# Residual adds and moments re-divided over VectorE, ScalarE and GpSimd in the ends of two Fourier layers; a re-ordered cold stage

## The chip, the cores and the metric

The kernel runs on one core of one Trainium2 chip. The metric is device time in microseconds (us) of one execution; medians of several executions are given. Every execution of every kernel was fast (granted clock 0.997 to 0.999). Engines: PE is TensorE, PEld its weight loads, DVE is VectorE, ACT is ScalarE, POOL is GpSimd, SP is SyncE.

A ratio of two kernels is the mean time of one kernel's fast runs over the mean of the other's fast runs of the same rounds. It is therefore not quite the ratio of the medians that are quoted beside it.

## The reference, cut to what matters

Four layers act on x of 2048 tokens by 640 features, alternating A, B, A, B:

```python
x = x + A(layernorm(x), w_r, w_i)     # rfft2, times complex weights, irfft2
x = x + B(layernorm(x), mem0, Wq, Wk, Wv, Wo)   # 32 heads, 64 segments of 32 tokens with a carried memory
x = x + A(layernorm(x), w_r, w_i)
x = x + B(layernorm(x), mem0, Wq, Wk, Wv, Wo)
```

The Fourier transforms of A are matrix products with constant tables. The change touches two places: the **cold stage**, in which the first A layer reads x and folds its layer norm into scaled tables, and the **token stage**, the end of each A layer, which is run twice. There the inverse transform is done for 16 rows (groups of 128 tokens), each row gets its residual and its layer norm, and the normalized rows are handed to B.

## The kernel before

The token stage's work for one row. `psg` is the spectrum product, `psy` the inverse transform; the residual is added by two matmuls with the identity:

```python
def spectrum_d(s0):
    psg = pp.tile([128, 2, 512], FP32, name="psg", tag="pg", bufs=3)
    ...                                    # 6 matmuls
    nc.scalar.copy(out=Gs[s0 % 3], in_=psg[:, :, 0:NF])

def tokens(s0):
    ...
    psy = pp.tile([128, 2, 512], FP32, name="psy", tag="pg", bufs=3)
    for a in range(2):
        nc.tensor.matmul(psy[:, a, 0:320], lhsT=g["ident"][:], rhs=x[:, s0, a * 320:(a + 1) * 320], start=True, stop=False)
    ...                                    # 4 matmuls of the inverse transform
    if s0 < 15:
        nc.scalar.copy(out=halves(x[:, s0, :]), in_=psy[:, :, 0:320])
    ...

def stats(s0):                             # two bn_stats and a bn_aggr on VectorE
    _ln_stats(nc, st[s0 // 2], mv[s0 // 2], x[:, s0, :], s0 % 2)
```

Two rows share one inverse square root. ScalarE takes Ln and Exp of the variances, then GpSimd refines the result in four small operations after adding epsilon:

```python
nc.scalar.activation(out=r0, in_=mv[:, :nt, 1], func=ACTF.Ln, bias=eps_t[:, 0:1])
nc.scalar.activation(out=r0, in_=r0, func=ACTF.Exp, scale=-0.5)
small.tensor_scalar_add(out=t, in0=mv[:, :nt, 1], scalar1=LN_EPS)
small.tensor_tensor(out=t, in0=t, in1=r0, op=ALU.mult)
small.tensor_tensor(out=t, in0=t, in1=r0, op=ALU.mult)
small.tensor_scalar(out=t, in0=t, scalar1=-0.5, scalar2=1.5, op0=ALU.mult, op1=ALU.add)
small.tensor_tensor(out=t, in0=t, in1=r0, op=ALU.mult)
```

In this text the *statistics* of a row are the two `bn_stats`, one for each half of it; the *aggregate* (`bn_aggr`) joins them to the *moments*, which are the row's mean and variance; the *inverse* is the inverse square root of the variance, and the *norm* is the operation that subtracts the mean and multiplies by the inverse. PSUM is the memory into which TensorE writes its products.

In the main loop the program fixes the order of the instructions of TensorE, ScalarE and VectorE (`manual_schedule`), and in the timelines below each engine works its queue off in order, whatever else is ready.

Of the kernel before, what the change touches and what calls it, by code (L numbers as in the profile page):

```python
# [19 lines left out]
S, D = 2048, 640  # L20
NF = 321
# [86 lines left out]
def _ln_inverse(nc, pool, mv, nt, eps_t, small):  # L108
    rs = pool.tile([128, 4], FP32, name="lnrs", tag="lnrs", bufs=3)
    nb = pool.tile([128, 4], FP32, name="lnnb", tag="lnnb", bufs=3)  # L110
    t, r0 = rs[:, :nt], nb[:, :nt]
    nc.scalar.activation(out=r0, in_=mv[:, :nt, 1], func=ACTF.Ln, bias=eps_t[:, 0:1])
    nc.scalar.activation(out=r0, in_=r0, func=ACTF.Exp, scale=-0.5)
    if small is nc.vector:
        small.scalar_tensor_tensor(out=t, in0=mv[:, :nt, 1], scalar=LN_EPS, in1=r0, op0=ALU.add, op1=ALU.mult)
        small.scalar_tensor_tensor(out=t, in0=t, scalar=-0.5, in1=r0, op0=ALU.mult, op1=ALU.mult)
        small.scalar_tensor_tensor(out=t, in0=t, scalar=1.5, in1=r0, op0=ALU.add, op1=ALU.mult)
        return rs, nb
    else:
        small.tensor_scalar_add(out=t, in0=mv[:, :nt, 1], scalar1=LN_EPS)  # L120
        small.tensor_tensor(out=t, in0=t, in1=r0, op=ALU.mult)
    small.tensor_tensor(out=t, in0=t, in1=r0, op=ALU.mult)
    small.tensor_scalar(out=t, in0=t, scalar1=-0.5, scalar2=1.5, op0=ALU.mult, op1=ALU.add)
    small.tensor_tensor(out=t, in0=t, in1=r0, op=ALU.mult)
    return rs, nb
# [7 lines left out]
def _ln_apply(nc, pool, mv, xin, xout, nt, eps_t, on_dve=False):  # L133
    rs, nb = _ln_inverse(nc, pool, mv, nt, eps_t, nc.vector)
    if on_dve:
        _ln_scale(nc, mv, rs, xin, xout, nt)
        return
    nc.vector.scalar_tensor_tensor(out=nb[:, :nt], in0=mv[:, :nt, 0], scalar=-1.0, in1=rs[:, :nt], op0=ALU.mult, op1=ALU.mult)
    for t in range(nt):
        nc.scalar.activation(out=xout[:, t, :], in_=xin[:, t, :], func=ACTF.Identity, scale=rs[:, t:t + 1], bias=nb[:, t:t + 1])  # L140
# [54 lines left out]
class LayerA:  # L195
# [71 lines left out]
    def cold_raw(self, x_src, s3):  # L267
# [9 lines left out]
        for a, b in ((0, 2), (2, 4), (4, 8), (8, 12), (12, 16)):  # L277
            nc.sync.dma_start(out=x[:, a:b, :], in_=r16(x_src)[:, a:b, :])
            if a in (4, 8):
                nc.sync.dma_start(out=T[:, 2 * a - 8:2 * a, :], in_=g["cd"]["cT"][:, 2 * a - 8:2 * a, :])  # L280
        groups = [(0, 4), (4, 8), (8, 12), (12, 14), (14, 16)]
        by_act = (3, 7, 11)
        pp = tc.alloc_tile_pool(name=f"{self.lname}_ps1", bufs=8, space=PSUM)

# [3 lines left out]

        def scales(q):
            a, b = groups[q]  # L290
            sl, v = slice(a, b), mv[:, a:b, 1]
            small = nc.gpsimd if q < 4 else nc.vector
            nc.scalar.activation(out=r0[:, sl], in_=v, func=ACTF.Ln, bias=g["eps"][:, 0:1])
            nc.scalar.activation(out=r0[:, sl], in_=r0[:, sl], func=ACTF.Exp, scale=-0.5)
            n = b - 1 if b - 1 in by_act else b
            small.tensor_scalar_mul(out=mn[:, a:n], in0=mv[:, a:n, 0], scalar1=-1.0)
            if n < b:
                small.tensor_scalar_mul(out=mn[:, n:b], in0=nm[:, n:b], scalar1=D ** 0.5)
            t, r = rs[:, sl], r0[:, sl]
            if small is nc.gpsimd:  # L300
                small.tensor_scalar_add(out=t, in0=v, scalar1=LN_EPS)
                small.tensor_tensor(out=t, in0=t, in1=r, op=ALU.mult)
            else:
                small.scalar_tensor_tensor(out=t, in0=v, scalar=LN_EPS, in1=r, op0=ALU.add, op1=ALU.mult)
            small.tensor_tensor(out=t, in0=t, in1=r, op=ALU.mult)
            small.tensor_scalar(out=t, in0=t, scalar1=-0.5, scalar2=1.5, op0=ALU.mult, op1=ALU.add)
            small.tensor_tensor(out=t, in0=t, in1=r, op=ALU.mult)
            small.tensor_copy(out=mh[:, sl, 0], in_=mn[:, sl])
            small.tensor_tensor(out=mh[:, sl, 1], in0=mn[:, sl], in1=mh[:, sl, 0], op=ALU.subtract)

        def stats(t):
            for hlf in range(2):
                nc.vector.bn_stats(out=st[:, t % 2, hlf, :], in_=x[:, t, hlf * 320:(hlf + 1) * 320])
            nc.vector.bn_aggr(out=mv[:, t, :], in_=st[:, t % 2, :, :])

        def scale_tables(q):
            for t in range(*groups[q]):
                nc.vector.tensor_scalar_mul(out=Ts[:, t, :], in0=T[:, t, :], scalar1=rs[:, t:t + 1])
# [27 lines left out]
        with tc.manual_schedule(engines={nc.tensor.engine, nc.scalar.engine, nc.vector.engine, nc.gpsimd.engine}):  # L346
            act_stats(3)
            for t in (0, 1, 2):
                stats(t)
            scales(0)  # L350
            self.tables(mirror=False)
            self.load_mirror(0)
            act_stats(7)
            for t in (4, 5):
                stats(t)
            scale_tables(0)
            ps0 = matmuls(0)
            stats(6)
            scales(1)
            self.load_mirror(1)  # L360
            act_stats(11)
            for t in (8, 9):
                stats(t)
            scale_tables(1)
            empties(0, ps0, "AA")
            ps1 = matmuls(1)
            stats(10)
            scales(2)
            empties(0, ps0, "  AAA")
            for t in (12, 13):  # L370
                stats(t)
            scales(3)
            empties(1, ps1, "AA")
            scale_tables(2)
            ps2 = matmuls(2)
            stats(14)
            stats(15)
            scale_tables(3)
            scales(4)
            empties(1, ps1, "  AAA")  # L380
            ps3 = matmuls(3)
            scale_tables(4)
            empties(2, ps2, "AAADD")
            empties(3, ps3, "AADAD")
            ps4 = matmuls(4)
            empties(4, ps4, "DADAD")
# [183 lines left out]
    def tokens(self, x_dst, xn_dst, handoff=None):  # L570
# [17 lines left out]
        nm = wk.tile([128, 1], FP32, name="lnnm", tag="lnnm")  # L588

        def tokens(s0):  # L590
# [5 lines left out]
            for a in range(2):  # L596
                nc.tensor.matmul(psy[:, a, 0:320], lhsT=g["ident"][:], rhs=x[:, s0, a * 320:(a + 1) * 320], start=True, stop=False)
            nc.tensor.matmul(psy[:, 0, 0:320], lhsT=Ti[:, s0, 0, :], rhs=G[:, 0, 0:320], start=False, stop=False)
            nc.tensor.matmul(psy[:, 0, 0:320], lhsT=Ti[:, s0, 0, :], rhs=G[:, 1, 0:320], start=False, stop=True)
            nc.tensor.matmul(psy[:, 1, 0:320], lhsT=Ti[:, s0, 0, :], rhs=G[:, 0, 320:0:-1], start=False, stop=False)  # L600
            nc.tensor.matmul(psy[:, 1, 0:320], lhsT=Ti[:, s0, 1, :], rhs=G[:, 1, 320:0:-1], start=False, stop=True)
            if s0 < 15:
                nc.scalar.copy(out=halves(x[:, s0, :]), in_=psy[:, :, 0:320])
            else:
                nc.scalar.activation(out=halves(x[:, s0, :]), in_=psy[:, :, 0:320], func=ACTF.Identity, accum_out=nm[:])
# [5 lines left out]
        def stats(s0):  # L611
            _ln_stats(nc, st[s0 // 2], mv[s0 // 2], x[:, s0, :], s0 % 2)

        def act_stats(s0):
            m, scr = mv[s0 // 2][:, s0 % 2, :], Gs[1].rearrange("p a b -> p (a b)")[:, 0:D]
            nc.scalar.mul(out=nm[:], in_=nm[:], mul=-D ** -1.5)
            nc.scalar.activation(out=scr, in_=x[:, s0, :], func=ACTF.Square, scale=D ** -0.5, bias=nm[:, 0:1], accum_out=m[:, 1:2])
            nc.gpsimd.tensor_scalar_mul(out=m[:, 0:1], in0=nm[:], scalar1=-D ** 0.5)

        def inverse(q, small):  # L620
            rs[q], _ = _ln_inverse(nc, wk, mv[q], 2, g["eps"], small)

        def norm(q):
            xno = xna[:, 2 * q:2 * q + 2, :]
            _ln_scale(nc, mv[q], rs[q], x[:, 2 * q:2 * q + 2, :], xno, 2)
            nc.sync.dma_start(out=xnd[:, 2 * q:2 * q + 2, :], in_=xno)

        with tc.manual_schedule(engines={nc.tensor.engine, nc.scalar.engine, nc.vector.engine}):
            moved, late = [], []
            for i in range(16 + 1):  # L630
                for f in moved:
                    f()
                moved = []
                if late:
                    late.pop(0)()
                last = i >= 13
                if i >= 2 and last:
                    stats(i - 2)
                if i >= 5 and i % 2 == 1:
                    norm((i - 5) // 2)  # L640
                if i >= 2 and not last:
                    stats(i - 2)
                if i < 16:
                    spectrum_d(i)
                if 1 <= i <= 16:
                    tokens(i - 1)
# [14 lines left out]
                if i >= 8 and i % 4 < 3:  # L661
                    n = i % 4
                    jobs = handoff.rows_out(handoff.rows_in(pp, xna, i // 4 - 2, 2 * n), n != 1 and i < 16)
                    if n == 1:
                        late = jobs
                    else:
                        moved = jobs
            act_stats(15)
# [274 lines left out]
class _BOut:  # L943
# [13 lines left out]
    def run(self, wk, oT_of, psx, first=(), n_first=0):  # L957
        nc = self.tc.nc
        for t in range(S // 128):
# [11 lines left out]
            if self.xnd is not None:  # L971
# [3 lines left out]
                _ln_apply(nc, wk, mv, xo, xno, 1, self.g["eps"], on_dve=True)  # L975
# [496 lines left out]
class _FastOut:  # L1472
# [10 lines left out]
    def run(self, x, lhs_of, psx, first, n_first, pa, xns, check, acc, flag_col):  # L1483
        nc, nxt = self.tc.nc, self.nxt
        early = {t: c for c, t in enumerate((3, 5) if nxt is not None else (3, 5, 7, 9, 11))}
        for t in range(16):
# [10 lines left out]
            else:  # L1497
# [4 lines left out]
                _ln_apply(nc, self.g["ln"], mv, x[:, t:t + 1, :], xns[t % 3].unsqueeze(1), 1, self.g["eps"], on_dve=True)  # L1502
# [169 lines left out]
def make_globals(ctx, tc, Wq, Wk, Wv, Wo, mem0):  # L1672
# [8 lines left out]
    nc.vector.memset(g["eps"][:], LN_EPS)  # L1681
    g["floor"] = sp.tile([128, 1], FP32, name="floor")
# [127 lines left out]
```

## Time and profile before

The kernel before takes 1558.79 us (three runs, 1558.63 to 1559.9).

| stretch | us | what is in it |
|---|---|---|
| cold stage | 26.6 | VectorE without a gap until its last scaled table |
| spectrum, not changed | 47.5 | TensorE |
| token stage, first and second | 42.4 each | TensorE early, three engines near full later |
| attention, not changed | 674.0, first | TensorE 99.9% busy |

First the operations of one inverse in the token stage (line, engine, operation, names, shapes, count; busy us and mean ns of one; idle time before), then VectorE's wait for their result (us in total, number of waits, longest; up to 107.1, that is without the wait of 0.71 before the norm of rows 12 and 13).

```profile
L120 POOL TENSOR_SCALAR lnrs<-lnmv 128x2 f32<-128x2 f32 x7 | 1.7, 241 | 20.1 <-DVE lnmv L105 20.1
L121 POOL TENSOR_TENSOR lnrs<-lnrs,lnnb 128x2 f32<-128x2 f32 x7 | 1.4, 196 | 6.8 <-ACT lnnb L113 6.2 <-ACT lnnm L616 0.7
...
L123 POOL TENSOR_SCALAR lnrs<-lnrs 128x2 f32<-128x2 f32 x7 | 1.3, 191 | 0.6
```

```profile
DVE A1tok_S L130 <- POOL lnrs L124: 3.4, 3, 2.1
```

### The profile page before, as it was taken

The page shows a single profiled execution, that of the slowest core. Times are in us where ns is not written, and L with a number is a line of the kernel's source. Part 1 is how long each engine was busy: PE and PEld are TensorE (multiplying, and loading weights), DVE is VectorE, ACT ScalarE, POOL GpSimd, SP SyncE. Part 2 cuts the span into 40 slices and gives each one's busy share as a digit, 9 for nine tenths or more (in the row PEclk, how much of TensorE's full clock was granted, in tenths as well). Part 3 has the DMA queues.
Part 4 walks back from the last instruction along what each step waited for, and adds up shares of the span by engine and source line. Part 5 has one row for each costly group of instructions (what it writes and reads, how often), then busy time and mean ns, then how long its engine had stood idle before and what let it go on. Part 6 is the DMA issues. An engine that isn't in the chain of part 4 may idle for free.

```text
span 1557.3 us, 36583 instructions
## 1 busy us (share of the span) xinstructions
PE 1531.2 (98%) x14482; PEld 1077.5 (69%) x14483; DVE 815.5 (52%) x2414; ACT 771.7 (50%) x2251; POOL 234.4 (15%) x327
## 2 busy tenths in 40 slices
PE   7999999999999999999999999999999999999998
PEld 5776666666666666777777776666666666667775
DVE  7873545665556555633367545655556545553111
ACT  5584555556555565511127655556555565562000
POOL 3520111112111121100034101112111121110000
PEclk9999999999999999999999999999999999999999
DMA  4681344444433433645114523443533434327241
GB/s 171 222 304 30 111 151 140 137 140 134 160 131 137 148 125 145 203 116 169 51 50 165 174 69 125 137 150 124 179 123 137 146 125 171 124 101 233 75 132 51
DMA packets 168694, 214.88 MB, mean 138 GB/s; under 512 B 8128, under 2 KB 134088, under 8 KB 168512
## 3 DMA queue, kind: packets, MB, share of 16 engines
q1 hardware_dynamic: 167936, 210.15, 41.0%
q8 instruction: 115, 1.88, 0.5%
q0 software_dynamic: 576, 2.30, 0.4%
q14 instruction: 67, 0.55, 0.1%
HBM read 167.32 MB, written 45.10 MB: 136 GB/s over the span
## 4 chain that ended last, share of the span: by engine, by line
PE 94%; DVE 2%; ACT 1%; DMA 1%; issue 1%; POOL 1%; SPq 0%; DVEq 0%; POOLq 0%; ACTq 0%
PE psv L1201 19%; PE psk L1135 18%; PE psx L1481 18%; PE psq L1135 18%; PE pso L1285 4%; PE pss L1211 4%; PE ab L427 2%; PE psg L585 1%; PE psl L1238 1%; PE psq L1159 1%; PE X L458 1%; PE psu L519 1%; PE psm L911 1%; DMA bB_S<-in_B_Wk_dram 1%; PE psg L1642 1%
## 5 line engine op out<-in xcount | busy, mean ns | idle before, releaser
L1135 PEld LDWEIGHTS <-bB_S 128*128 128x128 bf16 x3180 | 261.7, 97 | 181.6 <-DMA bB_S<-in_B_Wk_dram 1.1
L1194 DVE CAST bB_S<-psk 128x495 bf16<-128x495 f32 (+3 forms) x320 | 191.8, 599 | 281.2 <-PE psk L1135 276.7
L1481 PE MATMUL psx<-Wo_sb,bB_S 128*128 128x320 bf16 x2048 | 288.7, 299 | 0.1
L1214 ACT ACTIVATE bB_S<-pss 128x269 bf16<-128x269 f32 (+5 forms) x576 | 208.4, 386 | 138.2 <-PE pss L1211 137.9
L1481 PEld LDWEIGHTS <-bB_S 128*128 128x128 bf16 x2048 | 196.8, 98 | 73.9 <-DVE bB_S L1299 0.7
L1179 ACT ACTIVATE bB_S<-psq 128x96 bf16<-128x96 f32 x300 | 152.4, 508 | 172.2 <-PE psq L1135 172.2
L1254 POOL TENSOR_TENSOR bB_S<-bB_S,bB_S 128x535 f32<-128x535 f32 x90 | 111.7, 1255 | 795.2 <-DVE bB_S L1246 762.2
L1299 DVE TENSOR_TENSOR bB_S<-pso,bB_S 128x480 bf16<-128x480 f32 (+1 forms) x320 | 193.1, 603 | 55.6 <-PE pso L1285 44.9
L1215 DVE TENSOR_TENSOR bB_S<-bB_S,maskf 128x269 bf16<-128x269 bf16 (+5 forms) x576 | 159.4, 290 | 114.4 <-ACT bB_S L1214 114.4
L1203 ACT CAST bB_S<-psv 128x512 bf16<-128x512 f32 (+1 forms) x288 | 162.6, 564 | 80.9 <-PE psv L1201 80.9
L1201 PE MATMUL psv<-bB_S,B1hT_S 128*128 128x256 bf16 x1360 | 168.8, 272 | 0.0
L1201 PE MATMUL psv<-bB_S,B2hT_S 128*128 128x256 bf16 x1360 | 168.8, 272 | 0.0
L1135 PE MATMUL psk<-B2hT_S,bB_S 128*128 128x495 bf16 (+3 forms) x800 | 164.2, 343 | 0.0
L1135 PE MATMUL psk<-B1hT_S,bB_S 128*128 128x495 bf16 (+3 forms) x800 | 164.2, 343 | 0.0
L1135 PE MATMUL psq<-B1hT_S,bB_S 128*128 128x495 bf16 (+5 forms) x780 | 156.1, 336 | 0.6 <-DMA bB_S<-in_B_Wk_dram 0.5
L1135 PE MATMUL psq<-B2hT_S,bB_S 128*128 128x495 bf16 (+5 forms) x780 | 156.1, 336 | 0.5 <-DMA bB_S<-in_B_Wk_dram 0.5
L1201 PEld LDWEIGHTS <-B2hT_S 128*128 128x128 bf16 x1360 | 129.8, 98 | 24.3
L1201 PEld LDWEIGHTS <-B1hT_S 128*128 128x128 bf16 x1360 | 129.8, 98 | 24.3
L1211 PE MATMUL pss<-bB_S 128*128 128x132 bf16 (+8 forms) x1152 | 137.5, 219 | 0.0
L1211 PEld LDWEIGHTS <-bB_S 128*128 128x128 bf16 x1152 | 95.4, 97 | 55.1
L1285 PE MATMUL pso<-bB_S,bB_S 128*128 128x132 bf16 (+8 forms) x1152 | 118.6, 219 | 0.2
L1285 PEld LDWEIGHTS <-bB_S 128*128 128x128 bf16 x1152 | 89.7, 98 | 32.2 <-DVE oTmf L1300 1.8
(293 smaller groups left out, 1422.0 us busy)
## 6 DMA issues: line engine op xcount, KB each, us to landing
bB_S<-Rd SPq DMA_DIRECT2D x124, 535.0 KB
oTx_d<-bB_S SPq DMA_DIRECT2D x60, 512.0 KB
bB_S<-oTx_d SPq DMA_DIRECT2D x46, 512.0 KB
bB_S<-in_B_Wq_dram SPq DMA_DIRECT2D x32, 320.0 KB
bB_S<-in_B_Wk_dram SPq DMA_DIRECT2D x32, 320.0 KB
bB_S<-in_B_Wv_dram SPq DMA_DIRECT2D x32, 320.0 KB
Wo_sb<-in_B_Wo_dram SPq DMA_DIRECT2D x4, 1280.0 KB
B1wv_S<-in_B_Wv_dram SPq DMA_DIRECT2D x10, 512.0 KB
```

The source lines that it names most:

```text
L1135: nc.tensor.matmul(ps, lhsT=w[:, ch, hh * 128:(hh + 1) * 128], rhs=src[:, ch, lo:hi], start=(ch == 0), stop=(ch == 4))
L1179: nc.scalar.mul(out=qv[:, :, 0:SEG], in_=x_view(ps, o, n)[:, :, 1:SW], mul=scale)
L1194: nc.vector.tensor_copy(out=KTs[h % 2][:, lo:hi], in_=ps[:, 0:hi - lo])
L1201: nc.tensor.matmul(ps[:, i * 256:(i + 1) * 256], lhsT=hT[:, ch, st.hcol((t + i) * 128):st.hcol((t + i) * 128) + 128], rhs=w["Wv"][:, ch, : ...
L1203: nc.scalar.copy(out=V[:, t:t + n, :].rearrange("p a b -> p (a b)"), in_=ps[:, 0:n * 256])
L1211: nc.tensor.matmul(ps[:, off - o0:off - o0 + hi - lo], lhsT=KT[:, t * 128:(t + 1) * 128], rhs=QT[:, lo:hi], start=True, stop=True)
L1214: nc.scalar.activation(out=E[:, 0:n], in_=ps[:, 0:n], func=ACTF.Exp)
L1215: nc.vector.tensor_tensor(out=P[:, o0:o0 + n], in0=E[:, 0:n], in1=bs.mask[:, o0:o0 + n], op=ALU.mult)
L1254: nc.gpsimd.tensor_tensor(out=acc, in0=acc, in1=part, op=ALU.add)
L1285: nc.tensor.matmul(pso[:, lo - q0:hi - q0], lhsT=V[:, t, (h % 2) * 128:(h % 2 + 1) * 128], rhs=P[:, off:off + hi - lo], start=(i == 0), st ...
L1299: nc.vector.tensor_tensor(out=oT.rearrange("p (r s j) -> p r s j", r=16, j=2)[:, :, s0:s0 + ns, :], in0=byclass(po), in1=rx, op=ALU.mult)
L1481: self.tc.nc.tensor.matmul(ps[:, 0:320], lhsT=lhs(h, k // 2), rhs=self.g["Wo_sb"][:, h, c0:c0 + 320], start=(h == 0), stop=(h == H - 1))
```

## The change: its intent, and the diff

The intent is to relieve TensorE where it is the bound. In six of the first seven rows VectorE adds the residual while it reads the product from PSUM, so the identity matmuls go. To make room on VectorE, the moments of rows 1, 3 and 6 go to ScalarE (a Square with a sum), Ln and Exp leave ScalarE for a power on GpSimd, and each aggregate of statistics is issued one operation later. Rows 0 to 6 run two steps behind their spectrum instead of one (the lag).

```diff
-def _ln_inverse(nc, pool, mv, nt, eps_t, small):        (the GpSimd branch)
-    nc.scalar.activation(out=r0, ..., func=ACTF.Ln, ...)
-    nc.scalar.activation(out=r0, ..., func=ACTF.Exp, scale=-0.5)
     small.tensor_scalar_add(out=t, in0=v, scalar1=LN_EPS)
+    small.tensor_tensor(out=r0, in0=t, in1=g["half"][:, 0:t.shape[1]], op=ALU.pow)
     ...                                                  (the four refining operations stay)
 def tokens(...):
+    LEAD, LAG, EARLY, LAST = 0, 7, 10, 10
+    ADDED, SQUARED = (0, 1, 2, 3, 4, 6), (1, 3, 6) + (15,)
-            for a in range(2):
+            for a in range(0 if by_dve else 2):
                 nc.tensor.matmul(psy[:, a, 0:320], lhsT=g["ident"][:], ...)
+            if by_dve and acc is None:
+                nc.vector.tensor_tensor(out=xr, in0=psy[:, :, 0:320], in1=xr, op=ALU.add)
+                flush()
+            elif by_dve:
+                nc.vector.scalar_tensor_tensor(out=xr, in0=psy[:, :, 0:320], scalar=1.0, in1=xr, ..., accum_out=acc)
+                flush()
+    def stats(s0):
+            if s0 in SQUARED:
+                act_stats(s0)
+            else:
+                flush()
+                ...                                       (two bn_stats)
+                pending.append(s0)                        (bn_aggr later, in flush)
+        turn = lambda s0: s0 + (2 if LEAD <= s0 < LAG else 1)
 def cold_raw(...):
-        by_act = (3, 7, 11)
+        by_act = (3, 7, 11, 13)
+        for i in range(WARM):                             (WARM = 96)
+            nc.tensor.matmul(idle[:, i % 4, :], lhsT=g["ones"][:], rhs=g["ones"][:], start=True, stop=True)
     ...   (the refining steps move from GpSimd to VectorE, two tables to ScalarE, the order is new)
```

## The prediction

> **What bounds the kernel now.** I read the page first, then the busy time by stretch, then the chain of waits and the timeline of the two stretches that the diff touches.
>
> ```profile
> PE 1531.2 (98%) x14482; PEld 1077.5 (69%) x14483; DVE 815.5 (52%) x2414; ACT 771.7 (50%) x2251; POOL 234.4 (15%) x327
> ...
> PE 94%; DVE 2%; ACT 1%; DMA 1%; issue 1%; POOL 1%; SPq 0%; DVEq 0%; POOLq 0%; ACTq 0%
> ```
>
> TensorE carries 94% of the chain. Most of it is the attention layers, which the diff does not touch. So the question is what share the touched stages have. From the busy time by stretch (us of the span, PE, PEld, DVE, ACT, POOL, clock, DMA share, GB/s):
>
> ```profile
> 0.00:26.56 26.56, 15.68 (x240) 15.09 (x242) 20.39 (x77) 16.80 (x42) 9.90 (x45) 1.00 0.67 244
> ...
> 74.04:116.42 42.38, 40.25 (x522) 30.52 (x522) 30.35 (x90) 35.96 (x76) 7.92 (x46) 1.00 0.84 291
> 116.42:790.39 673.97, 673.15 (x6287) 468.77 (x6288) 341.82 (x1078) 330.47 (x1001) 78.70 (x67) 1.00 0.40 129
> ...
> 837.86:880.14 42.28, 40.26 (x523) 30.50 (x521) 30.38 (x90) 35.96 (x76) 7.92 (x46) 1.00 0.85 291
> ```
>
> The cold stage is 26.6 us and the token stage 42.4 us, twice. Together 111 us, 7% of the span; a 2% gain (31 us) would need over a quarter of it to vanish. That alone nearly settles the verdict; what follows is about microseconds.
>
> Inside the token stage the busy time splits the first eight rows (74.04 to 88.30) from the rest (88.30 to 104.55):
>
> ```profile
> 74.04:88.30 14.26, 14.26 (x106) 9.75 (x106) 7.17 (x23) 11.98 (x22) 2.00 (x10) 1.00 0.86 304
> 88.30:104.55 16.25, 15.60 (x136) 11.11 (x134) 15.22 (x43) 14.44 (x30) 4.06 (x20) 1.00 0.80 298
> ```
>
> Early, TensorE never rests while VectorE is half idle. Later VectorE is busy 15.22 of 16.25 us, ScalarE 14.44, TensorE 15.60: three engines near full, each able to stop the others. In the chain of waits it is TensorE to 92.8, then ScalarE, GpSimd and VectorE take turns:
>
> ```profile
> 92.86 0.69 ACT A1x_S L603
> 93.55 0.68 ACT B1hT_S L1610
> ...
> 94.36 0.31 ACT lnnb L112
> ...
> 95.04 0.20 POOL lnrs L121
> ...
> 96.10 0.81 DVE A1tok_S L130 x2
> ```
>
> The cold stage is VectorE's. From the arrival of x at 7.79 to its last scaled table at 22.34 it has hardly a gap, and then ScalarE still has nine PSUM copies in a row to do (timeline):
>
> ```profile
> 20.86 3.83 ACT L265 CAST A1YT_S<-ps 128x512 bf16<-128x512 f32 x9
> ```
>
> **What the Trainium skill says.** "TensorE: Matmul & The Clock Gate", Part 1, says an array that was idle runs at half clock until about 3.4 us of activity. The trace agrees in size: the first twelve 128-column matmuls take 1.60 us, a later twelve of the same line 0.83. The 96 added dummy matmuls aim at this. "VectorE: DVE Perf Modes", the perf-mode tier table, says a two-tensor operation with a PSUM operand runs at one element per cycle; the trace has 0.82 us for 128x642 from PSUM (line 443), so I use 0.81 for the new residual adds of 128x640. "Perfetto Trace Analysis", Optimization Strategy, says a repeating gap can mean too few buffers; here three PSUM buffers are shared by two products per row, which is the place where a late VectorE add would stop TensorE. On GpSimd's power operation I found no page with a cost, and the trace has none; its other two-element operations take 0.19 to 0.24 us, with 0.08 between.
>
> **Token stage, part by part.** Six rows lose two identity matmuls. The chain has them at 0.27 per pair: 6 x 0.27 = 1.65 us off TensorE, in the part where TensorE is the bound. A row costs it 0.83 (spectrum) + 0.55 = 1.38 instead of 1.65. For VectorE it adds 6 x 0.81 = 4.9 us and takes away the moments of rows 1, 3 and 6: 3 x 1.04 = 3.1 (two statistics 0.89, then the aggregate; cadence 1.04). ScalarE loses six copies (6 x 0.69 = 4.1) and seven Ln/Exp pairs (7 x 0.5 = 3.5), and gains three squares (3 x 0.93 = 2.8).
>
> Does the add come in time? A row's PSUM buffer is wanted again 1.38 us after its last matmul; an add takes 0.81, but behind a pair of statistics 0.95 + 0.81 = 1.76. So some of the saving returns as waits. Walking VectorE's queue from the first add, at 74.04 + 3.3 = 77.3: six adds 4.9, statistics of four rows at 0.96 = 3.8, two norms of two rows at 0.80 = 1.6, small copies 0.3: 10.6 without a gap, plus about 1 us of waiting for GpSimd's inverse of rows 0-3, which needs ScalarE's square and then six operations of 0.28 = 1.7. It ends at 89.0. The last add then holds TensorE about 0.4 us at row 8. Before, VectorE was at the same place (first copy of transposed rows) at 90.43. Gain so far **1.3 us**, of 1.65.
>
> Later rows: VectorE is nearly solid, so its work decides. It does the same norms and copies, row 6's moments have gone earlier, and delaying the aggregate saves the short wait behind the second statistic: by the timeline the pair ends, 0.03 later the aggregate starts, and the next statistic 0.13 later, so about 0.09 per row; seven to eight rows, **0.6 us**. ScalarE no longer carries the Ln/Exp pairs (0.25 per row), so the stretch at 92.8-96.1 should lose its ScalarE part.
>
> End: from the last product the old chain is row 15's copy with sum, Ln and Exp of rows 12-13 (0.5), scale, square, Ln, Exp, two norms. The 0.5 leaves ScalarE, but VectorE's norm of rows 12-13 still waits for GpSimd's six operations; I count 0.2. After the last norm (109.4) come 6.5 us of first-guess products and copies until the attention starts at 116.4; these only shift. The chain names a weight load of 4.72 us there; TensorE's queue waits on ScalarE's last PSUM copy, ended 116.28, so I do not count the load as a bound.
>
> Sum: 1.3 + 0.6 + 0.2, less 0.3 of new buffer waits = **1.8 us per stage, 3.6 for both**.
>
> **Cold stage.** VectorE gains the three inverse steps of each group: 5 x 0.6 = 3.0 against 1.4 of small operations now in the last group, +1.6. It loses row 13's statistics (1.04), two scaled tables (0.37), and 9 x 0.09 = 0.8 by delayed aggregates: net -0.6. Part of the new work fills the 0.74 us it now waits for x rows 4-7. ScalarE gains row 13's moments (1.7) and two tables (0.5) before the last Ln/Exp pair, and there it comes late: I put that pair at 21.7 instead of 20.42, the last table near 23.2 instead of 22.34. But three of the nine copies are then already done (3 x 0.52 = 1.5), so the tail after the last table shrinks from 4.2 to about 3.1 us. End near 26.3, against 26.56. The warm-up matmuls speed the first group by about 1.5 us, but that group is not on the path (its result waits for ScalarE). I take **0.6 us**, a little more than the walk.
>
> Total: 3.6 + 0.6 = 4.2; 1558.8 - 4.2 = **1554.6 us**.
>
> **Rivals.** (1) VectorE becomes the bound in the early rows too, and the saved matmuls come back as PSUM waits: for it speak 15.22 of 16.25 later, and the 1.76 against 1.38 above; against it, 7.17 of 14.26 now. Then each stage gains 0.5: near 1557.2. (2) GpSimd's inverse is slow: if the power operation costs 1 us rather than 0.2, each norm comes 0.8 later; GpSimd has room (4.06 of 16.25), so early this is slack, but rows 12-13's inverse is near the end: 0.5 to 1 us per stage, 1556. (3) Freed ScalarE lets TensorE run the later rows without gaps (0.65 us of idle plus row 15's wait): 2.8 per stage and 1.5 in the cold stage: 1551.7. (4) A transfer hides it all: DMA share is 0.84 in the stage, but no compute waits for weights in the chain before 109; I give this little.
>
> **Range and chances.** 1551.6 to 1557.4 spans rivals 1 to 3. Only one core runs and the three runs differ by 1.3 us. Over 2% either way needs 31 us from 111: 1% faster, 1% slower, 98% within.
>
> **What would show it.** Right: in the early rows TensorE's spacing falls from 1.65 to 1.4-1.5 us, adds take about 0.81, the first copy of transposed rows on VectorE starts 1.3 us earlier after the stage's start, the two token stages end 1.5 to 2 us shorter, the cold stage ends near 26. Wrong: TensorE waiting on the adds for more than 1 us in a stage, a power operation over 0.5 us, ScalarE's last Ln in the cold stage after 22.5 us, or the attention stretches changing by over 1 us.

## The result, and the profile after

The changed kernel takes **1554.54 us** (four runs, 1554.24 to 1554.74), the kernel before 1559.09 in the same rounds (four runs). The ratio is 0.997, 95% interval 0.9953 to 0.9987: the same within 2%, 4.5 us less. The changed page, and its busy time by stretch (us, then busy us of PE, PEld, DVE, ACT, POOL, clock, DMA share, GB/s):

```profile
PE 1535.5 (99%) x14554; PEld 1081.3 (70%) x14555; DVE 816.6 (53%) x2418; ACT 764.9 (49%) x2229; POOL 246.0 (16%) x337
...
PE 92%; DVE 4%; POOL 1%; ACT 1%; issue 1%; DMA 0%; ACTq 0%; DVEq 0%; POOLq 0%
```

```profile
0.00:25.74 25.74, 22.64 (x336) 21.43 (x337) 19.79 (x81) 18.84 (x48) 6.91 (x29) 1.00 0.70 251
73.22:114.01 40.79, 39.05 (x511) 29.35 (x510) 31.22 (x90) 31.72 (x62) 15.18 (x59) 1.00 0.89 303
114.01:787.71 673.70, 673.01 (x6287) 468.69 (x6288) 341.81 (x1078) 330.28 (x1001) 78.78 (x67) 1.00 0.39 129
835.18:875.95 40.77, 39.04 (x512) 29.36 (x510) 31.21 (x90) 31.71 (x62) 15.16 (x59) 1.00 0.87 300
```

The cold stage lost 0.82 us (26.56 to 25.74), the first token stage 1.59 (42.38 to 40.79), the second about as much, and the first attention stretch 0.27. The spectrum in between takes 47.48 us in both. The token stage's busy time tells what was moved: ScalarE 35.96 to 31.72, TensorE 40.25 to 39.05, GpSimd 7.92 to 15.18.

The page's chain of waits gives VectorE 4% instead of 2%. The surprise is in the chain of the early rows. Here TensorE was never interrupted before; now it runs through GpSimd (start us, us, what):

```profile
79.48 0.83 ACT A1tok_S L666 x2
80.31 0.07 issue
80.38 0.24 POOL lnrs L124
80.62 0.07 issue
80.70 0.74 POOL lnnb L125
...
82.63 0.44 POOL lnnm L663
83.09 0.12 ACT A1tok_S L666
83.21 0.62 issue
83.83 0.20 ACT A1tok_S L666
84.02 0.07 issue
84.09 0.24 POOL lnrs L124
84.33 0.07 issue
84.40 0.73 POOL lnnb L125
...
86.04 0.20 POOL lnrs L129
86.27 0.45 DVE A1tok_S L134
```

Read it as a story. The square of row 1 on ScalarE ends (80.31), GpSimd inverts rows 0 and 1 in six operations, of which L125 is the power. Only then does it get to the small scaling for row 3 (82.63), whose input VectorE had ready at 81.76: GpSimd works its queue in order here. ScalarE squares row 3, GpSimd inverts rows 2 and 3 from 84.09 to 86.24, and VectorE can normalize them at 86.27. The groups and the waits of the token stage say how much that is:

```profile
L125 POOL TENSOR_TENSOR lnnb<-lnrs,half 128x2 f32<-128x2 f32 x7 | 5.1, 728 | 0.6
L124 POOL TENSOR_SCALAR lnrs<-lnmv 128x2 f32<-128x2 f32 x7 | 2.0, 289 | 5.9 <-DVE lnmv L658 4.3 <-ACT A1tok_S L666 1.4
L126 POOL TENSOR_TENSOR lnrs<-lnrs,lnnb 128x2 f32<-128x2 f32 x7 | 1.4, 196 | 0.5
```

```profile
DVE A1tok_S L134 <- POOL lnrs L129: 3.1, 4, 1.1
```

The power takes 0.73 us, where the other operations of the inverse take 0.19 to 0.29 on average, and VectorE waits 3.1 us for GpSimd in four places. "Perfetto Trace Analysis", section GPSIMD Engine Instruction, advises to time such instructions by the spacing of their starts rather than by their reported duration. Done so (84.40 to 85.21), the power takes 0.81 us of the chain, the addition before it 0.31 and each of the others 0.27 to 0.28, so the reading stands.

How late the early rows are as a whole is read from VectorE's first copy of transposed rows, before and after. The stages start at 74.04 and 73.22 by the chain, so it comes 16.39 us after the start before, and 15.48 after:

```profile
90.43 1.32 DVE L1610 COPY B1hT_S<-pstr 128x480 bf16<-128x480 bf16 x2
```

```profile
88.70 0.69 DVE L1676 COPY B1hT_S<-pstr 128x480 bf16<-128x480 bf16 x1
```

### The profile page after: what moved, and what is told of

Same layout as the page of the kernel before. It is cut to its first block, busy times and chain, and to the rows that moved or that the text cites. A ratio compares the mean times of both kernels' runs of the same rounds, so it can differ in the third digit from the quotient of the medians.

```text
span 1552.9 us, 36725 instructions
## 1 busy us (share of the span) xinstructions
PE 1535.5 (99%) x14554; PEld 1081.3 (70%) x14555; DVE 816.6 (53%) x2418; ACT 764.9 (49%) x2229; POOL 246.0 (16%) x337
## 4 chain that ended last, share of the span: by engine, by line
PE 92%; DVE 4%; POOL 1%; ACT 1%; issue 1%; DMA 0%; ACTq 0%; DVEq 0%; POOLq 0%
PE psv L1267 19%; PE psk L1201 19%; PE psx L1547 18%; PE psq L1201 18%; PE pso L1351 4%; PE pss L1277 4%; PE ab L449 2%; PE psl L1304 1%; PE psq L1225 1%; PE X L480 1%; PE psu L541 1%; DVE lnst L650 1%; PE psm L977 1%; PE psg L1708 1%; PE psvb L1640 1%
```

## The experiments

**Theory** after the result: the early rows are held by the chain from ScalarE's square through GpSimd's six operations to VectorE's in-order norm, so the saved matmuls show only in part. **Rivals**: VectorE's own work holds the early rows (then a shorter GpSimd chain gives nothing); the freed ScalarE earned the gain, not the saved matmuls; or the cold stage earned it.

Every kernel below ran in five rounds (the change in four), was correct against the reference, and stayed within 2% of the kernel before; all ratios and intervals are against the kernel before of the same rounds. "Token stage" is the time from the stage's first spectrum product to the attention's first query product in the timeline, first and second layer. It starts some 0.15 us earlier than the boundaries from the chain used above. The change, "token stage alone" and "no warm-up" have the same token stage and show 40.72 to 40.95, so differences of 0.2 us between two profiles mean nothing.

| kernel | median us | ratio [95%] | token stages us |
|---|---|---|---|
| before | 1559.04, 1559.03, 1558.93, 1558.93 | | 42.54, 42.55 |
| the change | 1554.54 | 0.9970 [0.9953, 0.9987] | 40.95, 40.93 |
| cold stage alone | 1557.69 | 0.9991 [0.9977, 1.0005] | 42.54, 42.53 |
| token stage alone | 1555.82 | 0.9979 [0.9966, 0.9993] | 40.78, 40.78 |
| no residual adds | 1556.57 | 0.9984 [0.9970, 0.9997] | 41.86, 41.88 |
| bare power | **1550.94** | 0.9948 [0.9934, 0.9962] | 39.12, 39.12 |
| bare power, no adds | 1553.75 | 0.9964 [0.9950, 0.9978] | 40.73, 40.75 |
| Ln and Exp kept | 1556.44 | 0.9980 [0.9966, 0.9993] | 41.91, 41.81 |
| aggregate at once | 1555.82 | 0.9978 [0.9964, 0.9992] | 41.89, 41.70 |
| no lag | 1552.37 | 0.9953 [0.9939, 0.9966] | 39.74, 39.72 |
| bare power, no lag | 1551.51 | 0.9953 [0.9940, 0.9967] | 39.38, 39.42 |
| bare power, cold too | 1551.45 | 0.9952 [0.9938, 0.9965] | 39.11, 39.11 |
| no warm-up | 1554.67 | 0.9973 [0.9960, 0.9987] | 40.93, 40.72 |
| moments on VectorE | 1559.07 | 1.0001 [0.9987, 1.0015] | 43.01, 42.99 |

### 1 and 2. Each stage alone

Edit of the first: the changed cold stage with the old token stage put back. Edit of the second: the reverse.

> New cold stage, token stage of the kernel before. My sizing (cold stage worth 0.6 to 0.8 us, the profile after has its end at 25.74 against 26.56) expects about 1558.2, 0.6 to 1.0 under before, and token stages of 42.4 us. The rival that the cold stage also speeds what follows (the first attention pass was 0.27 us shorter) expects 1.1 or more.

> New token stage, cold stage of before. If the two parts simply add, this is 3.2 to 3.5 us under before (1555.6), with token stages of 40.8 us; if they depend on each other, the two separate gains do not sum to 4.4.

Measured: 1557.69 and 1555.82 against 1559.04, so 1.35 and 3.22 us. The sum, 4.57, is the whole gain (4.5), so within the noise the two parts do not disturb each other. The first interval includes 1, so the cold part's size is not sure by time alone. Its profile ends the cold stage at 25.75 us. Over all profiles the new cold stage ended at 25.46 to 26.34 and the old at 26.21 to 26.56, so single profiles scatter by nearly a microsecond there. The ten profiles whose new cold stage is that of the change average 25.76, the two with the old one 26.39. The token stages are steadier and are what the rest compares.

### 3. The adds undone

```diff
-ADDED, SQUARED = (0, 1, 2, 3, 4, 6), (1, 3, 6) + (15,)
+ADDED, SQUARED = (), (1, 3, 6) + (15,)
```

> The change, but the residual of all rows stays on TensorE (identity matmuls) and ScalarE copies out; lag, squares, power and delayed aggregate stay. My theory (the saved identity matmuls are worth 0.9 us of each stage, the rest of 1.6 comes from ScalarE and VectorE being relieved) expects about 1.8 us over the change: 1556.3. The rival that the matmuls are the whole gain (1.65 each) expects 1557.8; the rival that VectorE is the bound in the early rows as well expects no loss or even a gain, as VectorE loses 4.9 us of adds per stage.

Measured: 1556.57, stages 0.93 longer. In this kernel moving the six residuals is worth 0.93 us per stage and not the 1.65 that TensorE no longer spends. The edit takes back three things at once: the identity matmuls (TensorE +1.65), ScalarE's six copies (+4.1) and VectorE's six adds (-4.9). The 0.93 is their net, and no run separates the matmuls from the freed ScalarE.

### 4. A shorter inverse on GpSimd

```diff
-    small.tensor_tensor(out=r0, in0=t, in1=g["half"][:, 0:t.shape[1]], op=ALU.pow)
-    small.tensor_tensor(out=t, in0=t, in1=r0, op=ALU.mult)
-    small.tensor_tensor(out=t, in0=t, in1=r0, op=ALU.mult)
-    small.tensor_scalar(out=t, in0=t, scalar1=-0.5, scalar2=1.5, op0=ALU.mult, op1=ALU.add)
-    small.tensor_tensor(out=t, in0=t, in1=r0, op=ALU.mult)
+    small.tensor_tensor(out=t, in0=t, in1=g["half"][:, 0:t.shape[1]], op=ALU.pow)
```

The run's result is correct without the refining steps, so after the power the kernel does not need them.

> The change, but GpSimd's inverse stops after the power operation: add and power, without the four refining operations. If GpSimd's inverse delays the norms (the profile after has VectorE waiting 3.1 us on it in a stage, 0.87 of it right before the norm of rows 12-13), the stage gets 0.3 to 1.0 us shorter, 1553.0 to 1554.0 in all, with row 12-13's norm starting about 0.9 us earlier. If these waits are slack, nothing changes. It also shows if the power operation is exact enough alone.

Measured: 1550.94, better than expected, and the fastest kernel: 3.6 us below the change and 8.1 below the kernel before. The stages are 1.82 us shorter. In the stage its chain of waits has no GpSimd in it; TensorE runs without a break from the start of the stage to 98 us. The piece at the second norm, where the change waited:

```profile
83.86 0.14 PE psy L621
83.99 0.14 PE psy L622
84.13 0.83 PE psg L603 x6
84.96 0.14 PE psy L619
85.10 0.14 PE psy L620
```

Before each product of a row (L619 to L622) stands the next spectrum product (L603), with nothing between. The one wait of VectorE for GpSimd that is left in the stage:

```profile
DVE A1tok_S L130 <- POOL lnrs L125: 0.2, 1, 0.2
```

VectorE's wait for GpSimd fell from 3.1 to 0.2 us in the stage, with no other edit. And the gain lies where the theory puts it. The stage starts at 73.38 by the chain, and the first copy of transposed rows comes 13.73 us later, not 15.48:

```profile
87.11 0.69 DVE L1672 COPY B1hT_S<-pstr 128x480 bf16<-128x480 bf16 x1
```

These are 1.75 of the 1.82 us. That decides between the theory and its rival: GpSimd's latency, not VectorE's work alone, held the early rows.

### 5. The adds undone, with the shorter inverse

> The shortened GpSimd inverse together with the residual left on TensorE (no adds on VectorE). If GpSimd's long inverse was what held the early rows of the change, then with it short TensorE is the bound (its chain is unbroken from 73.38 to 98.2 us) and leaving out the adds costs the whole 1.65 us per stage: 3.3 over the run with the short inverse, about 1554.2. If the adds' worth does not depend on the inverse, it costs 2.0, as it did in the change itself: 1552.9.

The edits are those of experiments 3 and 4 together. Measured: 1553.75, between the two cases expected, and stages 40.73 and 40.75, that is 1.62 above experiment 4. (The time is 2.8 us longer and not 3.2, because in the two profiles the cold stage ended 0.33 us earlier without the adds.) With the chain out of the way moving the residuals is worth 1.62 us, the size of the 1.65 that it takes off TensorE. The sum of the prediction was right in kind: the saving was there, and GpSimd's chain held back 0.7 us of it.

### 6. Ln and Exp kept on ScalarE

```diff
+    nc.scalar.activation(out=r0, in_=v, func=ACTF.Ln, bias=g["eps"][:, 0:1])
+    nc.scalar.activation(out=r0, in_=r0, func=ACTF.Exp, scale=-0.5)
     small.tensor_scalar_add(out=t, in0=v, scalar1=LN_EPS)
-    small.tensor_tensor(out=r0, in0=t, in1=g["half"][:, 0:t.shape[1]], op=ALU.pow)
```

> The change, with the inverse's start value again from ScalarE (Ln and Exp) and the four refining steps on GpSimd, as before; all else of the change stays. My prediction had the power operation as a relief of ScalarE worth 0.2 us at the end of each stage: expects 0.4 or more over the change, 1555.0. The rival from the run with the short inverse (GpSimd's chain of 2.2 us is the bound, and Ln and Exp on ScalarE are shorter than 0.73 of power) expects less than the change: about 1553.5 to 1554.3.

Measured: 1556.44, stages 0.9 us longer. The power is slow, and still moving the pair off ScalarE gains about 0.9 us per stage. Two things are seen in its waits: VectorE waits 3.9 us for GpSimd instead of 3.1, because Ln and Exp queue behind ScalarE's copies and squares before GpSimd may go on (it waits 7.8 us for the Exp), and TensorE waits 1.0 us for ScalarE's spectrum copies:

```profile
DVE A1tok_S L135 <- POOL lnrs L130: 3.9, 5, 1.5
PE psy L623 <- ACT A1tok_S L609: 0.6, 1, 0.6
PE psy L624 <- ACT A1tok_S L609: 0.4, 1, 0.4
```

### 7. The aggregate at once

```diff
                 pending.append(s0)
+                flush()
```

> The change, but in the token stage each aggregate follows its two statistics at once, as before. My step (0.09 us per row off a nearly solid VectorE, 0.6 per stage) expects 1.0 to 1.2 over the change: 1555.6. In the profile after, the late rows gained only 0.3 us in all, so the rival (the delayed aggregate in the token stage gives nothing or costs, since the norms wait for it) expects no change within 0.2.

Measured: 1555.82, stages 0.94 and 0.77 longer. By these profiles delaying the aggregate is worth 0.86 us per stage; the device time is 1.28 longer, 0.64 per stage (that profile's cold stage ended 0.28 us earlier). Either way the prediction's 0.6 is confirmed in size. Its account, a short wait saved in each row of a queue with no slack, fits but was not tested apart.

### 8 and 9. No lag, with the long and with the short inverse

```diff
-LEAD, LAG, EARLY, LAST = 0, 7, 10, 10
+LEAD, LAG, EARLY, LAST = 0, 0, 10, 10
```

> The change, but every row follows its spectrum by one step, as before. In the change the two-step lag gives ScalarE and VectorE 1.38 us more per product; without it TensorE should wait for ScalarE's copy (0.69) and VectorE's add (0.81) of the same row: a gap of about 0.15 to 0.4 us in each of the six rows, 2 to 4 us over the change in all, 1557.5. If GpSimd's chain is the bound of the early rows anyway, the lag can even delay the norms, and it costs under 0.5.

Measured: 1552.37, stages 1.21 us **shorter**. This is the opposite of the main expectation: the lag costs time. The second case had the sign, that the lag can delay the norms, but under 0.5 us. The timelines show how. VectorE in the changed kernel first, then without the lag, from the first norm to the second (start us, us, operation):

```profile
82.58 0.80 DVE L134 TENSOR_SCALAR A1tok_S<-A1x_S,lnmv,lnrs 128x640 bf16<-128x640 bf16 x2 [0.69 <-POOL lnrs L129]
...
83.45 0.82 DVE L630 TENSOR_TENSOR A1x_S<-psy,A1x_S 128x640 bf16<-128x640 f32 x1
...
84.30 0.89 DVE L650 BATCH_NORM_STATS2 lnst<-A1x_S 128x6 f32<-128x320 bf16 x2
...
86.27 0.45 DVE L134 TENSOR_SCALAR A1tok_S<-A1x_S,lnmv,lnrs 128x640 bf16<-128x640 bf16 x1 [1.08 <-POOL lnrs L129]
```

```profile
82.14 0.79 DVE L134 TENSOR_SCALAR A1tok_S<-A1x_S,lnmv,lnrs 128x640 bf16<-128x640 bf16 x2
...
83.01 0.87 DVE L650 BATCH_NORM_STATS2 lnst<-A1x_S 128x6 f32<-128x320 bf16 x2
...
84.37 0.89 DVE L650 BATCH_NORM_STATS2 lnst<-A1x_S 128x6 f32<-128x320 bf16 x2 [0.25 <-ACT A1x_S L636]
...
85.17 0.81 DVE L633 SCALAR_TENSOR_TENSOR A1x_S<-psy,A1x_S 128x640 bf16<-128x640 f32 x1
...
86.03 0.75 DVE L134 TENSOR_SCALAR A1tok_S<-A1x_S,lnmv,lnrs 128x640 bf16<-128x640 bf16 x2
```

With the lag VectorE has one add and one pair of statistics to do between the two norms and then waits 1.08 us. Without it the next row's add was already done before the first norm (at 81.40), and two pairs of statistics and a further add fit in the same time: the wait for GpSimd is filled with work. The third norm starts at 89.79 instead of 91.52 us.

Does this stand by itself, or only while the inverse is long?

> The change with both edits at once: GpSimd's inverse reduced to an addition and the power, and no row delayed by a second step. Each alone gained: 3.6 us and 2.2 us against the changed kernel. If the lag only cost time because it brought the norms later than GpSimd's long chain already did, then with the short chain nothing is left to gain and the time is that of the short chain, 1551 to 1553, stages about 39.1. If the lag's cost is independent of the chain, the gains add: about 1548.7, stages about 37.9. If the lag becomes useful once the chain is short (TensorE then waits for VectorE's adds), it is slower than the short chain alone, above 1552, with waits of TensorE for VectorE's adds in the early rows.

Measured: 1551.51, stages 39.38 and 39.42, 0.26 and 0.30 longer than with the lag. So the gains of experiments 4 and 8 do not add; they are two cures for the same wait. With the long inverse the lag costs 1.2 us per stage; with the short one it seems to be worth about 0.3, which is little more than two profiles of the same stage differ by. The time lies in the range of the first case expected. The small gain of the lag points towards the third, but the TensorE waits for adds that this case named are not there, so whether and how the lag gains these 0.3 us is not shown.

### 10. The bare power in the cold stage too

```diff
 def logs(q):
-    nc.scalar.activation(out=r0[:, sl], in_=mv[:, sl, 1], func=ACTF.Ln, ...)
-    nc.scalar.activation(out=r0[:, sl], in_=r0[:, sl], func=ACTF.Exp, scale=-0.5)
 def scales(q):
-    (three nc.vector.scalar_tensor_tensor)
+    small.tensor_scalar_add(out=t, in0=v, scalar1=LN_EPS)
+    small.tensor_tensor(out=t, in0=t, in1=g["half"][:, 0:b - a], op=ALU.pow)
```

> The short chain in the token stage, and the same two GpSimd operations in the cold stage in place of ScalarE's Ln and Exp and VectorE's three refining steps. If VectorE's and ScalarE's busy time bounds the cold stage, taking 3.0 us from VectorE and 2.5 from ScalarE ends it 1 us or more earlier: about 1549.5. If what counts there is the latency from a group's last moments to its scaled tables, which GpSimd's two operations of about 0.9 us do not shorten by much, it is unchanged: 1550.5 to 1551.2, cold end near 25.7.

Measured: 1551.45 against experiment 4's 1550.94: nothing gained, though VectorE lost fifteen operations and ScalarE ten. VectorE's timeline at the end of that stage, and GpSimd's:

```profile
21.07 0.21 DVE L316 BATCH_NORM_AGGREGATE A1xn_S<-A1xn_S 128x2 f32<-128x12 f32 x1
22.45 0.42 DVE L327 TENSOR_SCALAR A1xn_S<-A1xn_S 128x128 bf16<-128x128 bf16 x2 [1.17 <-POOL A1xn_S L304]
```

```profile
16.30 1.05 POOL L304 TENSOR_TENSOR A1xn_S<-A1xn_S,half 128x4 f32<-128x4 f32 x1
...
21.68 0.73 POOL L304 TENSOR_TENSOR A1xn_S<-A1xn_S,half 128x2 f32<-128x2 f32 x1
```

VectorE waits 1.17 us for the last power; in the change the last tables are scaled at 22.22, here at 22.45. The stage ends at 26.25, not near the 25.7 expected, but within the scatter of the change's own cold stage. At that point what counts is the time from the last moments to the tables, and the freed engines have nothing to fill it with.

### 11. No warm-up matmuls

```diff
-WARM = 96
+WARM = 0
```

> The change without its 96 warm-up matmuls. The prediction put the first group's matmuls off the path of the cold stage: then the time is that of the change, 1554.5 within 0.3, although the first twelve matmuls take about 1.6 us again instead of 0.83. If those matmuls hold the copies behind them, the cold stage ends 0.5 to 1.5 us later: 1555 to 1556.

Measured: 1554.67, the time of the change. The first twelve matmuls take 1.55 us again, not 0.83:

```profile
8.49 1.55 PE L345 MATMUL ps<-A1xn_S,A1x_S 128*128 128x128 bf16 x12 [8.49 <-DVE A1xn_S L334]
```

The warm-up does what it is for, and it is off the path: the cold stage ends at 25.81.

### 12. The moments back on VectorE

```diff
-ADDED, SQUARED = (0, 1, 2, 3, 4, 6), (1, 3, 6) + (15,)
+ADDED, SQUARED = (0, 1, 2, 3, 4, 6), (15,)
```

> The change with the moments of rows 1, 3 and 6 back on VectorE (two statistics and an aggregate, 1.04 us each, in place of ScalarE's square and GpSimd's two small operations). If VectorE is near full in the token stage, 3.1 us more work on it lengthens the stage by 1 us or more: 1556.5 to 1558, stages 42 to 42.5. If GpSimd's chain holds the early rows, taking its two small operations for each of these rows and the wait for ScalarE's square away shortens it there, and VectorE had slack while it waited: about 1554 to 1555, stages 40.5 to 41.2. My theory, that GpSimd's chain held the early rows but VectorE bounds the later ones where only row 6 matters, expects +0.3 to +0.8 per stage: near 1555.5.

Measured: 1559.07, stages 2.06 us longer, slower than any of the three cases expected: the whole gain is gone. My theory's +0.3 to +0.8 per stage fell. Even in the early rows VectorE has no slack to speak of when it has both the adds and all the moments. "Perfetto Trace Analysis", section Optimizing Scalar/DVE Operations, says that with a saturated VectorE it may make sense to move work to ScalarE; here moving three rows' moments is worth 2.06 us per stage, the largest single part. The busy time of the first eight rows and of the rest, then the waits:

```profile
73.20:86.70 13.50, 13.40 (x97) 8.76 (x96) 9.57 (x25) 7.71 (x13) 2.69 (x8) 1.00 0.87 298
86.70:102.60 15.90, 13.29 (x115) 9.60 (x116) 14.57 (x42) 11.15 (x18) 7.58 (x29) 1.00 0.88 304
```

```profile
DVE A1tok_S L134 <- POOL lnrs L129: 3.0, 3, 1.4
PE pstr L1661 <- DVE A1tok_S L134: 1.9, 2, 1.7
```

In the second window TensorE works 13.29 of 15.90 us, where the changed kernel's had 15.43 of 15.94; it waits 1.9 us for VectorE's norms. VectorE's busy share in the early window, 9.57 of 13.50, hides this: of the idle 3.9 us, 2.95 end with the stage's first product and nearly all the rest is waiting for GpSimd. From its first add on VectorE has nothing free but those waits.

### What the parts add up to

Undoing one part at a time lengthens a stage by 0.93 (adds), 2.06 (moments), 0.92 (Ln and Exp) and 0.86 (aggregate), and shortens it by 1.21 (lag): 3.56 in sum, while the whole change gains 1.59 to 1.62. The parts are not independent: the lag and the long inverse hurt through the same wait, and that the adds fit only because the moments left VectorE is likely, though no run undoes both. The stage's other reorderings (norms placed after the products in the early steps, statistics before the norms from step 10 instead of 13, hand-off copies held back) were not undone alone, so what they are worth is open. A single undo measures a part in the company of all the others.

## Why the prediction was right or wrong

**The time was right** (1554.6 against 1554.54), and so was the argument: the change touches 111 of 1558 us, and the untouched stretches stayed (attention 673.97 to 673.70, spectrum 47.48 in both). **But its parts were not all right**, and that it came out to a tenth of a microsecond is luck. The gain was 4.5 us and not 4.2, from a kernel before at 1559.1 and not 1558.8. Each token stage gained 1.6 and not 1.8; the cold stage 0.8 and not 0.6 by one profile; the first attention stretch 0.3, which the sum did not have.

- **Early rows, 1.3 us: over-sized.** VectorE's first copy of transposed rows starts 15.48 us after the stage's start instead of 16.39: 0.91 gained. The walk put it at 89.0, 14.96 after the start; that is a gain of 1.43, of which the sum took 1.3 (and took off 0.3 for buffer waits without a place). The step that failed is the walk of VectorE's queue, "plus about 1 us of waiting for GpSimd's inverse of rows 0-3, which needs ScalarE's square and then six operations of 0.28 = 1.7". The first two waits were 0.69 + 1.08 = 1.8 us, not about 1, because one of the six operations is the power with 0.73 us and the inverse takes 2.15 us (84.09 to 86.24), and because row 3's scaling stands behind the first inverse in GpSimd's queue. Experiments 4 and 5 show that the rest of the sum held: with the short inverse moving the residuals is worth 1.62 us of 1.65.
- **TensorE's spacing and the adds: right.** The first undisturbed rows come every 1.38 us (76.32, 77.70, 79.08) after 1.66 before, and adds take 0.82. TensorE's recorded waits for the adds are 0.35 and 0.24 us in the stage, near the 0.4 and 0.3 counted.
- **Late rows, 0.6, and the end, 0.2: placed wrongly.** From that first copy to the start of ScalarE's copy of the last product (row 15) the gain is only 0.1 us; from there to the end of the last norm it is 0.58 (4.84 to 4.26). The two together are 0.7 of the 0.8 predicted. That the aggregate's delay is worth some 0.6 per stage was confirmed (0.64 to 0.86 in experiment 7); that Ln and Exp leaving ScalarE would be worth 0.2 at the end only was too little (0.92 in the whole stage, experiment 6). The lag, which the sum did not price, took 1.2 back (experiment 8).
- **Cold stage, 0.6: right in size.** 0.82 by the profile, 0.6 by the averages of experiment 1. The prediction's own walk gave 0.26 (26.3), and the 0.6 was a guess above it. The last Ln and Exp pair started at 21.06 (predicted 21.7), the last table ended at 22.64 (predicted 23.2, before 22.34), and the tail after it was 3.1 us as predicted, although the prediction's 4.2 less 1.5 makes 2.7. The warm-up was off the path, as said.
- **After the last norm, 6.5 us that only shift: right.** It is 7.0 in both kernels, counted to the first query product (109.4 to 116.4 is 7.0 too; the 6.5 was a slip). In the change the wait that ends last there is VectorE's copy out of PSUM (L1646). In the kernel before it was the weight load after all: it landed at 116.39, 0.11 us after the PSUM copy that the prediction took for the bound.
- **Rival 1, VectorE the bound early**: not alone in the change as built, but it was closer than the prediction made it. With the moments undone VectorE has no slack left, and the time is 1559.07.
- **Rival 2, a slow GpSimd inverse**: half right. The power is slow, 0.73 us, beyond the limit of 0.5 set for "wrong". What failed is "early this is slack": it was read from GpSimd's busy share (4.06 of 16.25, a figure of the later rows), which says nothing about the latency of a chain that an in-order VectorE waits for. The loss was early, not at the end: of the 1.82 us that the short inverse gains, 1.75 lie before the first copy of transposed rows.
- **Rival 3**, at 1551.7, is about where the kernel goes once that chain is short (1550.94), but its reason, a freed ScalarE, is not what the short chain changed.

## What to carry to other kernels

Judge an engine that answers small requests by the time from request to answer, not by its busy share, and look at which in-order queue stands still meanwhile. Where a wait cannot be shortened, give the waiting engine work to do in it: a pipeline lag that looks like relief can push that work behind the wait. When a change has many parts, undo each one alone: here one part cost 1.2 us per stage inside a change that gained 1.6, and dropping four leftover refining operations gained more than most of the rest.

## What the Trainium skill lacked or had wrong

- "GPSIMD Engine Reference" (and no other page that I found) gives no cost for the power operation. The runs show 0.73 us for 128x2 and 1.05 us for 128x4 f32; from these two, an estimate of 0.16 us per column and 0.4 us fixed.
- The same page, section 3.1, compares GpSimd and VectorE at 2048 elements and has no figure for tiny operations, which are what a norm's scalars need. The runs show averages of 0.19 to 0.29 us for 128x2, and starts every 0.27 to 0.31 us in a dependent chain, so that an inverse of six operations, one of them the power, takes 2.15 us.
- "Perfetto Trace Analysis", section Identifying the Most-Contended Engine, sends the reader to the engine with the highest occupancy. In the early rows that alone would have led to TensorE (busy 13.09 of 13.44 us) and not to GpSimd (4.65), whose shortened chain gained 1.8 us per stage. The page is not wrong, since it goes on to follow the gaps of that engine to what blocks it, but it does not warn that an engine of low occupancy can be the link to shorten.
- "TensorE: Matmul & The Clock Gate" lacks nothing here: what its Part 1 says of an idle array's half clock agrees in size (1.55 to 1.60 us cold against 0.83 warm for twelve matmuls). Only the clock column of the profiles does not show it: it reads 1.00 over the cold stage in both kernels.
